# Weight tiles shared by two batches, low halves on VectorE, high halves of P on ScalarE, decoding moved behind attention

## The chip, the core and the metric

The kernel runs on one core of one Trainium2 chip. A time is the device time of one execution in microseconds (us). The profile adds one profiled execution: its span runs from the first to the last instruction, and its times are the ones that a sum can be made from. Engines are named as in the profile: PE (TensorE matmul), PEld (its weight loads), DVE (VectorE), ACT (ScalarE), POOL (GpSimd), SP (SyncE, which here issues every DMA).

## What is computed

Four batches of 448 positions go through three layers: causal attention with 12 heads of width 64; a low-rank mix over positions and a two-layer MLP of width 768 to 3072 to 768, with a residual; four small attention experts, of which each position uses two.

```python
scores = scale * q @ k.T; scores = where(causal mask, -1e9, scores)
x = softmax(scores) @ v                         # 4 batches, 12 heads, 448 x 64
u = x + (x.T @ U @ V).T                         # rank 32 over the 448 positions
x = u + relu(u @ w_ch1) @ w_ch2                 # 768 x 3072 and 3072 x 768
logits = x @ w_gate                             # 4 experts, 2 are kept for each position
out = sum over kept e of w[e] * (softmax(causal(x wq[e] (x wk[e]).T)) @ (x wv[e])) @ wo[e]
```

The inputs arrive as 64-bit floats.

## The kernel before, in words

**Numbers in two halves.** A value is kept as a high and a low fp16 half, and a product takes three matmuls (high·high, high·low, low·high; `PASS`). A unit of MLP work is one such product of 448 columns: 18 matmuls for one 128-row weight tile and one batch.

**Attention** (`attention(b)`) takes a batch in six pairs of heads. For a pair: scores on PE, a fused scale, mask and row maximum on DVE (the rows `CUSTOM_DVE_ANT_0` in the profile, `ISA` in the order), the exponential on ACT, the split of P into halves (`softmax`: the high half by a copy that `HIGH` gives to ACT or DVE for each of the four row blocks, the low half by a POOL subtraction), two DMA transposes, P·V on PE, another split and transpose, and the low-rank product (`lowrank`). That last one ends, for the pair, in a DVE instruction of 128x448 on a PSUM bank; the twelfth of these ends the attention of batches 0 and 1 and serves as a mark below.

**Weights.** The 48 MLP tiles (4 groups `g` of 6 first-layer and 6 second-layer tiles) come in as 64-bit floats, 768 KB each. `weight_tile(i, first)` with `first` decodes one: three DVE instructions of 128x768 on the integers (one TENSOR_SCALAR, two SCALAR_TENSOR_TENSOR), a square sum on ACT, a norm through a small matmul on PE, the high half on ACT, the scaled tile on ACT, the low half in two pieces of 384 columns on POOL, and a store of both halves to `W16` in device memory. Later uses load 384 KB from `W16`. Tiles live in a ring of `NW` slots; raw tiles in two buffers, decoded ones in three.

**The MLP** (`mlp(g, b)`) multiplies one group of tiles with one batch. The hidden values have one buffer, `HID`. Its PSUM banks are two ("f") until the experts' weights are made, three after.

**Order.** `ORDER` is the program order: `a` attention, `m` a batch and a group, `e` the experts of a batch. The instructions are only recorded. `Program.issue` then lists them, engine by engine, with a table of costs: of the instructions whose inputs are ready it takes the one with the smallest key. Attention and decoding have keys that grow with the pair (`HT` is half a pair; `first_key(i)` for tile `i`), MLP products have the large key `FILL`, so that they fill gaps, and evictions are `URGENT`. The result is a fixed order on each engine. Until `WARM_END` in its own reckoning it also places matmuls of zeros (line 953) where it sees PE idle. Every queue runs in order, SP's too, where loads, stores and transposes stand behind each other.

Of the kernel before, what the change touches and what calls it, by code (L numbers as in the profile page):

```python
# [30 lines left out]
HIGH = ("act", "act", "dve", "dve")  # L31
# [11 lines left out]
WARM_START, WARM_END, WARM_GAP = 3000.0, 130000.0, 100.0  # L43
NW = 19
# [3 lines left out]
ORDER = "a0 a1 m00 m01 m02 m03 e0 a2 m10 m11 m12 m13 e1 a3 m20 m21 m22 m23 e2 m30 m31 m32 m33 e3"  # L48
# [4 lines left out]
class Program:  # L53
# [7 lines left out]
    def __init__(self):  # L61
        self.ops = []
        self.key = 0.0
        self.group_op = None
        self.state = {}
        self.near = {}
        self.pitch = {}
        self.idle = None

# [54 lines left out]
    def cost(self, name, method, outs, ins, kw):  # L124
        o = outs[0]
        n = 1
        for c in o.shape[1:]:
            n *= c
        if name == "pe":
            f = 4.0 if ins[0].dtype == F32 else 1.0  # L130
            c = f * max(n / 2.4 + 2.5, 36.0)
            self.work = c * (ins[0].shape[0] / 128.0) * (o.shape[0] / 128.0)

            return c * (0.62 if HD in (o.shape[0], ins[0].shape[0]) and n >= C else 1.0)
        ptr = sum(x.free_size() == 1 and n > 1 for x in ins)
        psum = any(a.space == bass.MemoryType.PSUM for a in outs + ins)
        if name == "act" and method == "dma_start":
            return 300.0
        if name == "act":
            src = 51.0 if ins[0].space == bass.MemoryType.PSUM else 94.0  # L140
            return src + n / 1.2 + 93.0 * (ptr + len(outs) - 1)
        if name == "dve":
            m = 1
            for c in ins[0].shape[1:] if ins else o.shape[1:]:
                m *= c
            m = max(m, n)
            fast = not psum and method in ("tensor_scalar", "tensor_copy", "memset")
            two = not psum and n > 32 and (fast or sum(x.free_size() > 1 for x in ins) > 1)
            return ((64.0 + (m / 2 if fast else m)) / 0.96 + 64.0 * ptr) * (1.2 if two else 1.0)
        if name == "pool":  # L150
            if method == "partition_all_reduce":
                return 374.0
            return 148.0 + 1.89 * n if method == "tensor_tensor" else 260.0 + 2.5 * n
        return 350.0 + outs[0].nbytes() / 292.0 if method == "dma_start_transpose" else 650.0

    def add(self, name, method, fn, a, k):
# [4 lines left out]
        self.work = 0.0  # L161
        cost = self.cost(name, method, outs, ins, k)
        data = 0.0
        if method.startswith("dma"):
            nbytes = max(x.nbytes() for x in outs + ins)
            data = nbytes / (185.0 if method == "dma_start_transpose" else 360.0)
# [21 lines left out]
        if self.group_op:  # L188
            op = self.ops[-1]
            op["calls"].append((fn, a, k))  # L190
            op["cost"] += cost
            op["work"] += self.work
            op["deps"] |= deps
        else:
            op = dict(eng=name, cost=cost, data=data, deps=deps, calls=[(fn, a, k)], key=self.key,
                      work=self.work)
            self.ops.append(op)
            if self.group_op is False:
                self.group_op = True

    def issue(self):
# [9 lines left out]
        bus = 0.0  # L211
# [7 lines left out]
        while done < len(ops):  # L219
# [56 lines left out]
def kernel(  # L276
# [19 lines left out]
    for name, size in [  # L296
        ("uh", 2 * KD * S * 2), ("ul", 2 * KD * S * 2), ("x3", 2 * KD * S * 4),
        ("ring", NW * 3072), ("rd", RD), ("hid", GF * 2 * S * 2),
        ("stage", 2 * 3584), ("vs", NP * 2048), ("vh", 4096), ("p", 3 * PW * 4), ("phl", 2 * NBLK * 128 * 2 * 2),
        ("pt", 3 * 20 * C * 2), ("xhl", 2 * 2048), ("xtr", 2048),  # L300
        ("wv", 2 * 3120), ("tst", 256),
        ("idf", 512), ("one", 512), ("mask", S * 2), ("u3", 2 * NC * 2 * R * 2), ("vst", S * 2), ("id", 256),
        ("tie", 64), ("zero", 64), ("sm", SM * 4),
    ]:
        layout[name] = total
        total += size
# [14 lines left out]
    BANKS = {"s": (0, 1), "o": (2,), "l": (3, 4), "m": (5, 6, 7), "f": (5, 6), "r": (7,), "x": (5, 6), "y": (2, 7), "b": (3, 4)}  # L321
# [16 lines left out]
    HID = view("hid", 0, 128, F16, GF * 2 * S).rearrange("p (f l s) -> p f l s", f=GF, l=2)  # L338
# [10 lines left out]
    def hslot(r, o):  # L349
        return view(r, o, C, F16, 2 * NBLK * 128)  # L350

    SLOTS = [
        (P32[0:3] + [pslot("x3", 10752), pslot("x3", 10752 + 4480)], PHL[0:2] + [hslot("uh", 5376), hslot("ul", 5376)]),
        (P32[0:3], PHL[0:2]), (P32[0:3], PHL[0:2]), (P32[0:3], PHL[0:2]),
# [130 lines left out]
    def softmax(terms, nes, pts, last=False, kind="s", first=False):  # L485
# [4 lines left out]
        elif first:  # L490
            ps, hs = SLOTS[0]
# [28 lines left out]
        for j in range(2):  # L520
# [14 lines left out]
            sp.dma_start_transpose(out=PT[pts[j]], in_=h16[j])  # L535
# [26 lines left out]
    def weighted(vs, pts, y, dst, coef=None, kind="o"):  # L562
        shares(y, coef)
        t = psum(kind)
        with prog.group():
            for i, (lp, lv_) in enumerate(PASS):
                for j in range(NC):
                    for h, (va, pt) in enumerate(zip(vs, pts)):
# [4 lines left out]
                           PT[pt][0:C, k:k + kc * (NC - 1 - j) + 1:kc],  # L573
# [37 lines left out]
    def attention(b):  # L611
# [6 lines left out]
        for p in range(NP):  # L618
# [6 lines left out]
            if p == NP - 1 and b + 1 < B:  # L625
                v_scale(b + 1)
            i = n % 2
            prog.key = HT * 2 * n
            softmax([[(QK[i][64 * j:64 * j + 64, 1], QK[i][64 * j:64 * j + 64, 0])] for j in range(2)], -0.125,
                    [(2 * n + j) % 3 for j in range(2)], first=b == 0)  # L630
            prog.key = HT * (2 * n + 1)
            weighted([VH[:, 2 * i + j] for j in range(2)], [(2 * n + j) % 3 for j in range(2)], X3[b][:, p], XHL[i])
# [19 lines left out]
    kept = [False]  # L652

    def weight_tile(i, first):
# [76 lines left out]
    def mlp(g, b):  # L731
        if b == 0:
            factors(g)
        ut = (UH[b], UL[b])
        for f in range(GF):
            early = g + b + f == 0
            t = psum("m" if kept[0] else "f")
            wt = [a.rearrange("p (k m) -> p k m", k=KD) for a in tiles[2 * GF * g + f]]
            prog.key = FILL - early
            product(t[:, 0:S], [(wt[lw][:, k], ut[lx][:, k]) for k in range(KD) for lw, lx in PASS])  # L740
            prog.key = URGENT
            act.activation(t[:, 0:S], t[:, 0:S], AF.Relu, scale=(RF if b else RF0)[:, g * GF + f:g * GF + f + 1])
            act.activation(HID[:, f, 0], t[:, 0:S], AF.Copy)
            dve.tensor_tensor(out=HID[:, f, 1], in0=t[:, 0:S], in1=HID[:, f, 0], op=ALU.subtract)
        cf, ct = CF[g % 2], CTS[g % 2]
        dve.tensor_scalar(ct, PRS[:, g:g + 1], 2.0 ** 54 / HCAP, PU[:, b:b + 1], op0=ALU.mult, op1=ALU.mult)
        dve.tensor_scalar(cf, PW2[:, g * GF:g * GF + KD], 2.0 ** 83, ct, op0=ALU.mult, op1=ALU.mult)
        for d in range(KD):
            t = psum("m" if kept[0] else "f")
            wt = [a.rearrange("p (k m) -> p k m", k=GF) for a in tiles[2 * GF * g + GF + d]]  # L750
            prog.key = FILL
            product(t[:, 0:S], [(wt[lw][:, f], HID[:, f, lx]) for f in range(GF) for lw, lx in PASS])
            prog.key = URGENT
            dve.scalar_tensor_tensor(out=X3[b][:, d], in0=t[:, 0:S], scalar=cf[:, d:d + 1], in1=X3[b][:, d],
                                     op0=ALU.mult, op1=ALU.add)
            if g == NG - 1:
                absmax(AMX[:, b * KD + d:b * KD + d + 1], X3[b][:, d])

    def experts(b):
# [3 lines left out]
        free = 3072 * next(i for i in range(NW - 5) if not held & set(range(i, i + 6)))  # L763
        if last:
            qo, vo, yo, xo = ("hid", 0), ("ring", free), ("hid", 7168), ("ring", free + 4096)
# [6 lines left out]
        if last:  # L772
            OST = [view("ring", free + 6144 + i * 1792, 128, F32, S) for i in range(6)]
        else:
            OST = [view("rd", 14848 + i * 1792, 128, F32, S) for i in range(2)]
        pts = (0, 1, 2, 3) if last else (0, 1, 0, 1)
# [126 lines left out]
    zero_pads(SLOTS[0][1])  # L903
# [25 lines left out]
    def first_key(i):  # L929
        return HT * (1 + 0.9 * i if i < 2 * GF else 12 + (i - 2 * GF) / 3)  # L930

    def group(b, g):
        for i in range(2 * GF * g, 2 * GF * (g + 1)):
            prog.key = URGENT if b else first_key(i)
            weight_tile(i, not b)
        mlp(g, b)
# [13 lines left out]
    for step in ORDER.split():  # L950
        kind, b = step[0], [int(c) for c in step[1:]]
        {"a": attention, "m": group, "e": moe}[kind](*b)
# [47 lines left out]
```

## Time and profile before

| | |
|---|---|
| median of 3 runs | 1176.02 us (1173.72 to 1176.1) |
| the profiled execution's own time | 1177.93 us |
| its span | 1176.2 us, so 1.7 us lie around it |
| busy in the span: PE, DVE, ACT, POOL | 1088.9, 678.1, 546.7, 371.3 us |
| mean granted TensorE clock | 0.967 of full speed |
| DMA | 192.57 MB, 164 GB/s on average |

A row by groups reads: line, engine, operation, output<-input, shapes, count | busy us, mean ns of one | idle us of the engine just before them. A row by stretches gives busy us of each engine with its count of instructions, the granted clock and the mean busy share of the 16 DMA engines. Nearly every instruction has line 250, because the recorder issues it there; so rows are told apart by engine, operation and shape.

### The profile page before, as it was taken

How to read it: one execution, taken by the hardware profiler on the slowest of the kernel's cores; microseconds unless marked ns; L12 is line 12 of the kernel's file. 1: busy time of each engine (PE TensorE's matmuls, PEld its weight loads, DVE VectorE, ACT ScalarE, POOL GpSimd, SP SyncE). 2: the span in 40 equal slices, each digit the busy share in tenths (PEclk: the TensorE clock that was granted, in tenths of full speed). 3: DMA queues.
4: the chain of work that ended last, by engine and by line, in shares of the span. 5: the costliest groups of instructions: out<-in, count | busy, mean ns of one | idle time of the engine just before them, and what ended most of it. 6: DMA issues, size and time to landing. Idle time of an engine off the chain costs nothing.

```text
span 1176.2 us, 18782 instructions
## 1 busy us (share of the span) xinstructions
PE 1088.9 (93%) x6888; PEld 571.7 (49%) x6888; DVE 678.1 (58%) x1831; ACT 546.7 (46%) x1317; POOL 371.3 (32%) x419
## 2 busy tenths in 40 slices
PE   7899969979988999999999999999999997899895
PEld 3454434434444455445555554455555544355452
DVE  8869888998889765665432555654224333111453
ACT  4755767676577544575412456652122323121142
POOL 3755755766453102454200034540000012000012
PEclk9999978998999999999999999999999998999998
DMA  7887888897786754998734349984443255331023
GB/s 195 208 195 245 211 199 242 260 229 206 230 265 222 239 189 112 213 231 200 175 108 120 96 107 216 234 180 118 122 121 108 82 131 112 125 121 54 1 40 87
DMA packets 220141, 192.57 MB, mean 164 GB/s; under 512 B 176304, under 2 KB 179504, under 8 KB 220048
## 3 DMA queue, kind: packets, MB, share of 16 engines
q1 hardware_dynamic: 220048, 191.36, 61.0%
q8 instruction: 54, 0.88, 0.3%
q14 instruction: 39, 0.32, 0.1%
HBM read 121.60 MB, written 26.74 MB: 126 GB/s over the span
## 4 chain that ended last, share of the span: by engine, by line
PE 65%; DVE 9%; issue 3%; ACT 3%; DMA 2%; POOL 2%; POOLq 0%; SPq 0%; DVEq 0%; ACTq 0%
PE bank L250 65%; DVE arena L250 9%; ACT arena L250 2%; POOL arena L250 2%; DMA arena<-in_v_dram 1%; DMA arena<-in_w_dram 0%; DMA arena<-in_we_dram 0%; DMA arena<-w 0%; ACT bank L250 0%; POOLq L995 0%; SPq L250 0%; DVEq L250 0%; ACTq L250 0%; POOLq L250 0%
## 5 line engine op out<-in xcount | busy, mean ns | idle before, releaser
L250 PE MATMUL bank<-arena 128*128 128x448 f16 (+12 forms) x6496 | 1006.5, 332 | 70.0 <-DVE arena L250 40.8
L250 PEld LDWEIGHTS <-arena 128*128 128x128 f16 (+4 forms) x5960 | 489.2, 106 | 489.8 <-issue 124.9
L250 POOL TENSOR_TENSOR arena<-arena 112x336 f16<-112x336 f32 (+6 forms) x408 | 369.1, 924 | 796.2 <-ACT arena L250 719.6
L250 ACT ACTIVATE arena<-arena 128x768 f16<-128x768 f32 (+10 forms) x671 | 376.6, 591 | 282.8 <-DVE arena L250 267.6
L250 DVE TENSOR_TENSOR arena<-bank,arena 128x448 f16<-128x448 f32 (+2 forms) x160 | 95.4, 600 | 215.2 <-ACT arena L250 183.4
L250 DVE CUSTOM_DVE_ANT_0 arena<-bank,arena 112x112 f32<-112x112 f32 (+4 forms) x280 | 125.7, 475 | 62.6 <-PE bank L250 55.1
L250 ACT ACTIVATE bank<-bank,arena 128x448 f32<-128x448 f32 x96 | 57.8, 603 | 222.8 <-PE bank L250 221.8
L250 DVE SCALAR_TENSOR_TENSOR arena<-bank,arena 128x448 f32<-128x448 f32 (+1 forms) x120 | 73.4, 614 | 148.0 <-PE bank L250 125.0
L250 DVE SCALAR_TENSOR_TENSOR arena<-arena 128x768 int32<-128x768 int32 (+5 forms) x159 | 154.9, 993 | 5.3 <-ACT arena L250 4.2
L250 ACT ACTIVATE arena<-bank 128x448 f16<-128x448 f32 (+2 forms) x160 | 82.6, 523 | 74.7 <-PE bank L250 72.8
L250 DVE TENSOR_SCALAR arena<-arena 128x1 f32<-128x1 f32 (+9 forms) x367 | 90.7, 267 | 20.1 <-ACT arena L250 9.7
L953 PE MATMUL bank<-arena 128*128 128x448 f16 x392 | 89.8, 376 | 13.4 <-DVE arena L250 12.4
L250 DVE CAST arena<-arena 112x336 f16<-112x336 f32 (+2 forms) x160 | 85.4, 547 | 2.1 <-PE bank L250 1.0
L250 PEld LDWEIGHTS bank<-arena 64*112 64x112 f32 (+5 forms) x536 | 49.4, 176 | 55.9 <-issue 18.9
L953 PEld LDWEIGHTS <-arena 128*128 128x128 f16 x392 | 39.1, 105 | 54.3 <-issue 25.9
L250 DVE TENSOR_REDUCE arena<-arena 128x1 f32<-128x448 f32 (+7 forms) x107 | 58.2, 546 | 9.5 <-DMA arena<-in_v_dram 5.2
L250 ACT ACTIVATION_READ_ACCUMULATOR arena<-arena 112x1 f32 (+1 forms) x304 | 57.0, 188 | 0.0
L250 ACT ACTIVATE arena<-bank,arena 64x128 f16<-64x128 f32 (+3 forms) x85 | 34.2, 405 | 44.6 <-PE bank L250 38.7
L250 DVE TENSOR_TENSOR arena<-arena 112x8 f16<-112x8 f32 (+4 forms) x69 | 24.6, 368 | 1.4
L250 DVE DVE_READ_ACCUMULATOR2_ANT arena<- 112x1 f32 (+1 forms) x280 | 22.7, 81 | 0.0
L250 DVE TENSOR_SCALAR arena<-bank 128x1 f32<-128x1 f32 x48 | 7.2, 149 | 12.8 <-PE bank L250 12.7
L250 DVE RECIPROCAL arena<-arena 112x8 f32<-112x8 f32 (+1 forms) x36 | 7.0, 195 | 0.7
(12 smaller groups left out, 13.6 us busy)
## 6 DMA issues: line engine op xcount, KB each, us to landing
arena<-w SPq DMA_DIRECT2D x162, 384.0 KB, 3.3
arena<-in_w_dram SPq DMA_DIRECT2D x48, 768.0 KB, 5.6
w<-arena SPq DMA_DIRECT2D x54, 384.0 KB, 3.1
arena<-in_qk_dram SPq DMA_DIRECT2D x24, 448.0 KB, 5.6
arena<-in_v_dram SPq DMA_DIRECT2D x24, 224.0 KB, 5.0
out_dram<-arena SPq DMA_DIRECT2D x24, 224.0 KB, 2.6
arena<-in_we_dram SPq DMA_DIRECT2D x6, 384.0 KB, 4.6
arena<-arena SPq DMA_TRANSPOSE x88, 4.6
```

What stands on the lines that cost most here:

```text
L250: fn(*a, **k)
L953: prog.idle = lambda: nc.tensor.matmul(bank[:, 7, 64:512], ZERO.to_broadcast([128, 128]), ZERO.to_broadcast([128, S]), start=True, stop=True)
```

## The change

Four things are changed together, and some sizes with them.

- **Two batches on one group of tiles.** `mlp(g, bs)` takes a list of batches, and a group is loaded or decoded once for steps that follow each other. In `ORDER` a step now reads group, then batches: `m00 m01` is group 0 for batch 0 and then batch 1, `m101` group 1 for both. `HID` gets a second buffer; to pay for it the ring shrinks from 19 to 15 slots.
- **Decoding behind attention.** `first_key` spreads the first 12 tiles over all twelve pairs and puts the other 36 after the last pair. Both attentions of batches 0 and 1 use the spare buffers for P. Matmuls of zeros may be placed until 210 in place of 130 (us, in the planner's reckoning). MLP steps recorded between attention 1 and expert step 0 use four PSUM banks, two of them shared with the scores.
- **The low half of a decoded tile** is formed on DVE by one SCALAR_TENSOR_TENSOR from the decoded tile (`split`, which was there already); the ACT pass that scaled the tile and the two POOL pieces go.
- **The high halves of P** are all copied on ACT.
- The planner's table of costs now keeps DVE instructions that read two operands from SBUF, or run at their fast rate, apart from POOL instructions.

```diff
-HIGH = ("act", "act", "dve", "dve")
+HIGH = ("act", "act", "act", "act")
-WARM_START, WARM_END, WARM_GAP = 3000.0, 130000.0, 100.0
-NW = 19
+WARM_START, WARM_END, WARM_GAP = 3000.0, 210000.0, 100.0
+NW = 15
-ORDER = "a0 a1 m00 m01 m02 m03 e0 a2 m10 m11 m12 m13 e1 a3 m20 m21 m22 m23 e2 m30 m31 m32 m33 e3"
+ORDER = "a0 a1 m00 m01 m101 m20 m30 e0 a2 m21 m31 e1 a3 m02 m12 m22 m32 e2 m03 m13 m23 m33 e3"
...
+            if o["port"]:
+                t = max(t, port)
+                port = t + cost
...
-        (P32[0:3], PHL[0:2]), (P32[0:3], PHL[0:2]), (P32[0:3], PHL[0:2]),
+        (P32[0:3] + [pslot("hid", 10752), pslot("hid", 10752 + 4480)], PHL[0:2] + SPARE, PT[0:3]),
+        (P32[0:3], PHL[0:2], PT[0:3]), (P32[0:3], PHL[0:2], PT[0:3]),
...
-        act.activation(hi, t, AF.Copy, scale=s)
-        act.activation(t, t, AF.Copy, scale=s)
-        for j in range(2):
-            cols = slice(384 * j, 384 * j + 384)
-            pool.tensor_tensor(out=lo[:, cols], in0=t[:, cols], in1=hi[:, cols], op=ALU.subtract)
+        split(hi, lo, t, s)
         sp.dma_start(out=W16[i], in_=both)
...
-    def mlp(g, b):
-        if b == 0:
+    def mlp(g, bs):
+
+        if 0 in bs:
             factors(g)
...
+        bank = "m" if kept[0] else "g" if started[0] else "f"
         for f in range(GF):
+            for b in bs:
...
     def first_key(i):
-        return HT * (1 + 0.9 * i if i < 2 * GF else 12 + (i - 2 * GF) / 3)
+        return HT * (1 + 2.0 * i if i < 2 * GF else 25 + (i - 2 * GF) / 3)
...
+    def group(g, bs):
+        if last_group[0] != g:
+            for i in range(2 * GF * g, 2 * GF * (g + 1)):
+                prog.key = URGENT if g in made else first_key(i)
+                weight_tile(i, g not in made)
...
+        mlp(g, bs)
```

SP's queue in the second half of attention 1 (batch 1), before. `in_w_dram` is a raw tile's load, `w<-arena` the store of a decoded one, the 128x20x112 transposes belong to P and the 128x8x128 ones to the low-rank step:

```order
L250 DMA arena<-in_v_dram 112x512
L250 DMA_TRANSPOSE arena<-arena 128x8x128
L250 DMA w<-arena 128x1536
L250 DMA arena<-in_w_dram 128x768
L250 DMA_TRANSPOSE arena<-arena 128x20x112
L250 DMA w<-arena 128x1536
L250 DMA arena<-in_w_dram 128x768
L250 DMA_TRANSPOSE arena<-arena 128x20x112
L250 DMA w<-arena 128x1536 x2
L250 DMA arena<-in_w_dram 128x768
L250 DMA arena<-in_qk_dram 128x896
```

And in the change, the last pairs of attention 1 and what follows them:

```order
L252 DMA_TRANSPOSE arena<-arena 128x20x112 x2
L252 DMA_TRANSPOSE arena<-arena 128x8x128
L252 DMA arena<-in_w_dram 128x768 x2
L252 DMA w<-arena 128x1536 x2
L252 DMA_TRANSPOSE arena<-arena 128x8x128
L252 DMA arena<-in_v_dram 112x512
L252 DMA arena<-in_w_dram 128x768
L252 DMA arena<-in_v_dram 112x512
L252 DMA w<-arena 128x1536
L252 DMA arena<-in_w_dram 128x768
L252 DMA w<-arena 128x1536
L252 DMA arena<-in_w_dram 128x768 x2
```

Most loads and stores of tiles moved from between the transposes to behind the last of them.

DVE in a pair of attention 1, before: an eviction of a hidden tile (TENSOR_TENSOR on a bank), two copies of P's high half (CAST with four dimensions), the small steps of a tile's norm (128x1) and of the row sums (112x8):

```order
L250 TENSOR_TENSOR arena<-bank,arena 128x448
L250 TENSOR_SCALAR arena<-arena 128x1
L250 CAST arena<-arena 112x2x3x56
L250 TENSOR_TENSOR arena<-bank,arena 128x448
L250 TENSOR_SCALAR arena<-bank 128x1
L250 TENSOR_SCALAR arena<-arena 112x8
L250 TENSOR_SCALAR arena<-arena 128x1
L250 RECIPROCAL arena<-arena 112x8
L250 CAST arena<-arena 112x2x4x56
```

In the change, in the last pair of attention 1 (ISA on a bank is the fused mask and maximum):

```order
L252 ISA arena<-bank,arena 112x448
L252 ISA arena 112x1
L252 SCALAR_TENSOR_TENSOR arena<-arena 128x768
L252 TENSOR_SCALAR arena<-arena 128x768
L252 TENSOR_SCALAR arena<-arena 112x8
L252 SCALAR_TENSOR_TENSOR arena<-arena 128x768
L252 SCALAR_TENSOR_TENSOR arena<-bank,arena 32x128
L252 TENSOR_TENSOR arena<-bank,arena 128x448
L252 RECIPROCAL arena<-arena 112x8
```

No copy of P stands on DVE any more, and a tile has three SCALAR_TENSOR_TENSOR of 128x768 where it had two.

ACT in a late pair of attention 1, in the change (112x2x3x56 and 112x2x4x56 are the high halves that DVE had; before, ACT had 128x768 passes of tiles and evictions of hidden tiles at this place):

```order
L252 ACTIVATE arena<-arena 112x2x2x56
L252 ACTIVATE arena<-arena 112x2x3x56
L252 ACTIVATE arena<-arena 112x448
L252 ACTIVATE arena<-bank,arena 64x128
L252 ACTIVATE arena<-bank,arena 32x128
L252 ACTIVATE arena<-arena 112x448
L252 ACTIVATE arena<-arena 112x2x3x56
L252 ACTIVATE arena<-arena 112x112
L252 ACTIVATE arena<-arena 112x2x4x56
L252 ACTIVATE arena<-arena 112x336
```

All four copies of P's high half now queue between the exponentials.

## Rows read from the trace of the kernel before

**Rows 1.** Page, busy time by engine, and DVE in 40 slices.
```profile
PE 1088.9 (93%) x6888; PEld 571.7 (49%) x6888; DVE 678.1 (58%) x1831; ACT 546.7 (46%) x1317; POOL 371.3 (32%) x419
DVE  8869888998889765665432555654224333111453
```

**Rows 2.** Stretches, before 345, to 432, to the end.
```profile
0.00:345.00 345.00, 294.97 (x1886) 151.28 (x1887) 294.81 (x776) 227.62 (x523) 204.95 (x209) 0.93 0.82 221
345.00:432.00 87.00, 79.85 (x426) 41.05 (x425) 67.35 (x147) 46.71 (x75) 20.66 (x20) 1.00 0.70 239
432.00:1177.00 745.00, 714.06 (x4580) 379.39 (x4577) 315.94 (x910) 272.36 (x722) 145.65 (x190) 0.98 0.51 128
```

**Rows 3.** Stretches of 25 us: one with MLP products alone.
```profile
1025.00:1050.00 25.00, 25.00 (x134) 12.92 (x132) 3.91 (x7) 5.44 (x10) 0.00 (x0) 1.00 0.40 124
```

**Rows 4.** The chain that ended last: start us, us, what.
```profile
391.40 159.20 PE bank L250 x1096
...
983.64 10.51 issue
...
1003.09 4.17 DMA arena<-w
```

**Rows 5.** PE groups by shape, 0 to 432.
```profile
L250 PE MATMUL bank<-arena 128*128 128x448 f16 x962 | 201.7, 361 | 20.1 <-DVE arena L250 18.3 <-ACT arena L250 1.6
L953 PE MATMUL bank<-arena 128*128 128x448 f16 x392 | 89.8, 376 | 13.4 <-DVE arena L250 12.4 <-DVE arena L897 1.0
...
L250 PE MATMUL bank<-arena 128*128 128x1 f32 x96 | 16.3, 239 | 5.3 <-ACT arena L250 4.8 <-DVE arena L250 0.2
```

**Rows 6.** DVE timeline: the mark, the twelfth low-rank instruction.
```profile
345.42 0.68 DVE L250 CUSTOM_DVE_ANT_0 arena<-bank,arena 128x448 f32<-128x448 f32 x1
```

**Rows 7.** DVE groups by shape, 0 to 345.
```profile
L250 DVE SCALAR_TENSOR_TENSOR arena<-arena 128x768 int32<-128x768 int32 x82 | 93.9, 1146 | 0.6
L250 DVE TENSOR_SCALAR arena<-arena 128x768 int32<-128x768 int32 x41 | 31.2, 760 | 7.0 <-DMA arena<-in_w_dram 3.7 <-POOL arena L250 2.8 <-issue 0.2
L250 DVE CAST arena<-arena 112x448 f16<-112x448 f32 x24 | 18.1, 758 | 0.0
...
L250 DVE CAST arena<-arena 112x336 f16<-112x336 f32 x24 | 14.1, 591 | 0.0
...
L250 DVE TENSOR_SCALAR arena<-arena 128x1 int32<-128x1 int32 x88 | 12.5, 144 | 0.4
...
L250 DVE TENSOR_TENSOR arena<-bank,arena 128x448 f16<-128x448 f32 x18 | 11.0, 616 | 3.1 <-ACT arena L250 3.0
```

**Rows 8.** DVE groups by shape, 398 to 426.
```profile
L250 DVE SCALAR_TENSOR_TENSOR arena<-arena 128x768 f16<-128x768 f32 x6 | 5.9, 1011 | 1.0 <-ACT arena L250 1.0
```

**Rows 9.** ACT groups by shape, 0 to 345.
```profile
L250 ACT ACTIVATE arena<-arena 128x768 f16<-128x768 f32 x79 | 69.5, 883 | 46.7 <-DVE arena L250 46.6
...
L250 ACT ACTIVATE arena<-arena 112x448 f32<-112x448 f32 x24 | 15.8, 660 | 4.0 <-DVE arena L250 4.0
L250 ACT ACTIVATE arena<-arena 112x336 f32<-112x336 f32 x24 | 13.6, 565 | 8.1 <-DVE arena L250 8.1
```

**Rows 10.** ACT groups by shape, 0 to 391: a high half of two blocks.
```profile
L250 ACT ACTIVATE arena<-arena 112x224 f16<-112x224 f32 x24 | 9.0, 375 | 0.0
```

**Rows 11.** POOL groups by shape, 0 to 345.
```profile
L250 POOL TENSOR_TENSOR arena<-arena 128x384 f16<-128x384 f32 x76 | 85.7, 1149 | 68.2 <-ACT arena L250 68.2
```

**Rows 12.** DMA, 0 to 345: queue, packets, MB, share of 16 engines; issues.
```profile
q1 hardware_dynamic: 83320, 75.73, 82.1%
...
arena<-in_w_dram SPq DMA_DIRECT2D x42, 768.0 KB, 5.7
...
arena<-arena SPq DMA_TRANSPOSE x36, 4.9
```

**Rows 13.** DMA, 600 to 660, where tiles alone are loaded.
```profile
q1 hardware_dynamic: 2435, 6.65, 37.3%
...
arena<-w SPq DMA_DIRECT2D x17, 384.0 KB, 3.1
```

**Rows 14.** DVE timeline: first instruction of a tile's decoding, first and last of seven.
```profile
325.45 0.56 DVE L250 TENSOR_SCALAR arena<-arena 128x768 int32<-128x768 int32 x1 [0.82 <-DMA arena<-in_w_dram]
...
375.66 0.54 DVE L250 TENSOR_SCALAR arena<-arena 128x768 int32<-128x768 int32 x1
```

More of the change, by code (lines that the diff above doesn't have):

```diff
@@ L68, in __init__ @@
         self.idle = None
+        self.port = False
     def engine(self, name, eng):
@@ L147, in cost @@
             fast = not psum and method in ("tensor_scalar", "tensor_copy", "memset")
-            two = not psum and n > 32 and (fast or sum(x.free_size() > 1 for x in ins) > 1)
-            return ((64.0 + (m / 2 if fast else m)) / 0.96 + 64.0 * ptr) * (1.2 if two else 1.0)
+            self.port = not psum and n > 1 and (fast or sum(x.free_size() > 1 for x in ins) > 1)
+            return (64.0 + (m / 2 if fast else m)) / 0.96 + 64.0 * ptr + 80.0 * (self.port and n > 32)
         if name == "pool":
@@ L337 @@
     DEC = [view("rd", 12288 + i * 3072, 128, F32, 768) for i in range(3)]
-    HID = view("hid", 0, 128, F16, GF * 2 * S).rearrange("p (f l s) -> p f l s", f=GF, l=2)
+    HID = [view("hid", i * 10752, 128, F16, GF * 2 * S).rearrange("p (f l s) -> p f l s", f=GF, l=2) for i in range(2)]
     QK = [view("stage", i * 3584, 128, F32, 2 * S).rearrange("p (t s) -> p t s", t=2) for i in range(2)]
@@ L483, in scaled_copy, with softmax @@
             dve.tensor_scalar(o, a, scale, None, op0=ALU.mult)
-    def softmax(terms, nes, pts, last=False, kind="s", first=False):
+    def softmax(terms, nes, pts, last=False, kind="s", slots=None):
         ps, hs = P32[0:3], PHL[0:2]
@@ new lines, in mlp @@
+            for b in bs:
+                early = g + b + f == 0
+                t = psum(bank)
+                wt = [a.rearrange("p (k m) -> p k m", k=KD) for a in tiles[2 * GF * g + f]]
+                prog.key = FILL - early
+                ut = (UH[b], UL[b])
+                product(t[:, 0:S], [(wt[lw][:, k], ut[lx][:, k]) for k in range(KD) for lw, lx in PASS])
+                hid = HID[b % 2]
+                prog.key = URGENT
+                act.activation(t[:, 0:S], t[:, 0:S], AF.Relu, scale=(RF if b else RF0)[:, g * GF + f:g * GF + f + 1])
+                act.activation(hid[:, f, 0], t[:, 0:S], AF.Copy)
+                dve.tensor_tensor(out=hid[:, f, 1], in0=t[:, 0:S], in1=hid[:, f, 0], op=ALU.subtract)
@@ new lines, in mlp @@
+        cf, ct = [[a[b % 2] for b in bs] for a in (CF, CTS)]
+        for i, b in enumerate(bs):
+            dve.tensor_scalar(ct[i], PRS[:, g:g + 1], 2.0 ** 54 / HCAP, PU[:, b:b + 1], op0=ALU.mult, op1=ALU.mult)
+            dve.tensor_scalar(cf[i], PW2[:, g * GF:g * GF + KD], 2.0 ** 83, ct[i], op0=ALU.mult, op1=ALU.mult)
+        for d in range(KD):
+            for i, b in enumerate(bs):
+                t = psum(bank)
+                wt = [a.rearrange("p (k m) -> p k m", k=GF) for a in tiles[2 * GF * g + GF + d]]
+                hid = HID[b % 2]
+                prog.key = FILL
+                product(t[:, 0:S], [(wt[lw][:, f], hid[:, f, lx]) for f in range(GF) for lw, lx in PASS])
+                prog.key = URGENT
+                dve.scalar_tensor_tensor(out=X3[b][:, d], in0=t[:, 0:S], scalar=cf[i][:, d:d + 1], in1=X3[b][:, d],
+                                         op0=ALU.mult, op1=ALU.add)
+                if g == NG - 1:
+                    absmax(AMX[:, b * KD + d:b * KD + d + 1], X3[b][:, d])
@@ L762, in experts @@
         held = {(ring_n[0] - 1 - i) % NW for i in range(NE)}
-        free = 3072 * next(i for i in range(NW - 5) if not held & set(range(i, i + 6)))
+        two = 3072 * next(i for i in range(NW - 1) if not held & {i, i + 1})
         if last:
-            qo, vo, yo, xo = ("hid", 0), ("ring", free), ("hid", 7168), ("ring", free + 4096)
+            qo, vo, yo, xo = ("hid", 0), ("ring", two), ("hid", 7168), ("ring", two + 4096)
         else:
@@ L772, in experts @@
         if last:
-            OST = [view("ring", free + 6144 + i * 1792, 128, F32, S) for i in range(6)]
+            OST = [view("hid", 10752 + i * 1792, 128, F32, S) for i in range(6)]
         else:
             OST = [view("rd", 14848 + i * 1792, 128, F32, S) for i in range(2)]
-        pts = (0, 1, 2, 3) if last else (0, 1, 0, 1)
+        pts = PT if last else PT[0:2] * 2
         ks, ko, kl = "xyy" if last else "sll" if b == B - 2 else "sol"
```

79 lines of the change are left out of this document (34 added, 45 removed).

## The prediction

> **What bounds the kernel now.** I read the page first, and in it the engines' shares beside DVE's 40 slices [rows 1]: PE is busy for 93% of the span, yet DVE, 58% on the whole, stands at eighths in the first third and at two to six tenths later. The kernel has regimes, and the mean tells of none. So the next view was the table by stretches [rows 2], cut at the mark: the twelfth low-rank instruction on DVE, at 345.4 [rows 6], which ends the attention of batches 0 and 1. Up to there DVE works 294.8 of 345 us, 85%, and the DMA engines 82%. PE's 295 us are padding in part: 392 products of zeros, 89.8 us [rows 5], and what PE waits for in these groups is mostly DVE. From 432 on, where the first value product of the experts stands, PE works 714 of 745 us and DVE 316.
>
> Is PE really full there? A stretch with nothing but MLP work has 134 products in 25.00 us [rows 3], 186.6 ns for 448 columns, at granted clock 1.00, the 2.4 GHz level. The chain [rows 4] says the same: from 391.4 it lies on PE for 159 us in one piece, and it leaves PE later for small pieces, such as 10.5 us of issue at 983.6 and 4.2 us of a weight load at 1003. The kernel is thus a first stage of 391 us bound by DVE and DMA, and then PE's own sum. Time is to be won only by ending the first stage earlier with no more left to PE.
>
> **The first stage, up to the mark.** I counted in the order of each program what stands ahead of the twelfth low-rank step. On DVE: 128x768 SCALAR_TENSOR_TENSOR 82 before and 44 now (30 of decoding, 14 new low halves), TENSOR_SCALAR 41 and 16, copies of P 48 and none, 128x1 steps 191 and 83, hidden and bank evictions down by 23. At the means of [rows 7]: 52 x 1.146 + 25 x 0.760 + 24 x (0.758 + 0.591) + 108 x 0.144 + 23 x 0.616 = 141 us go. The new low half has the price of the same operation from f32 to f16 halves, 1.011 [rows 8]: 14 us come. Net 127; since DVE's means overlap (count times mean over all its groups is 340 for 295 busy), 110 to 127 of busy time, and DVE falls from 295 to 168 to 185.
>
> ACT loses 86 of its 128x768 passes at 0.883 [rows 9], and gains the 48 copies of P's high half. Half-width copies cost 0.375 there [rows 10]; the full exponential of the same shape costs 0.565 to 0.660 [rows 9]; I take 0.565 of these ends as the mean of the two widths, 27 us. With its evictions gone too, ACT falls from 228 to about 170. POOL loses the 76 pieces of 128x384, 86 of its 205 us [rows 11]; nobody waits for that unless ACT and DVE are idle, so I cost it at nothing, hidden behind both.
>
> DMA: 82.1% of 345 is 283 us of all 16 engines [rows 12]. In the stretch where tiles alone are loaded, 17 loads of 384 KB take 37.3% of 60 us [rows 13], 1.32 us each, so 2.63 for a raw tile of 768 KB. In SP's queue 25 raw loads and 24 stores move from ahead of the last low-rank transpose to behind it (the 42 raw loads of [rows 12] become 16 or 17): 25 x 2.63 + 24 x 1.32 = 97 us, and DMA falls to 186. These transfers stood between the transposes of P in the same queue, which are 36 of 4.9 us [rows 12] and do not change in number.
>
> PE: MLP-shaped products ahead of the mark fall from 552 to 156, but zeros ahead of it grow from 392 to some 465. At 0.210 and 0.229 us each (201.7 / 962 and 89.8 / 392 [rows 5]) the rest of PE's 295 was 295 - 116 - 90 - 7 (44 norms of 0.17 that move) = 82. Now: 82 + 33 + 106 = 221, or, with both at 0.187 [rows 3], 198. The zeros were meant for gaps, but they stand in order, and now they are half of what PE does there.
>
> So DMA asks 186, DVE up to 185, PE 198 to 221. At the pace of before, where the busiest reached 0.855 of the stage, 186 gives 217 and 198 gives 232. The floor is 198, without any wait. At 0.774, DVE's share between 345 and 432 [rows 2], DMA's 186 would give 240. I take **225** for the mark, in place of 345, with 198 and 240 as its ends: 19 us for each of the twelve pairs of heads, where it was 29.
>
> **From the mark to the first value product.** The price of that gain stands here: 36 tiles are decoded behind attention, where only a few were. Up to that value product the order has 966 MLP-shaped products before (962 in the trace, [rows 5]) and 1383 now; after the mark that leaves 1383 - 156 = 1227, x 0.1866 = 229, and with 36 norms at 0.17 [rows 5], 235. PE was busy 79.85 of 87 us between 345 and 432, and 0.958 from 432 on [rows 2]. I take 0.95, as products for two batches on one tile give PE twice the work for each decoded tile: **247**, with ends 235 and 256. DVE's load here is 32 tiles of about 4.5 us (0.760 + 2 x 1.146 + 1.011 and small steps), 144, and some evictions, under 190 of 247.
>
> **From the value product to the end.** Now 744 us (1176.2 - 432). The products brought forward, 1383 - 966 = 417, are gone from here: 417 x 0.1866 = 78, which leaves **666**. Loads of decoded tiles fall from 162 to 138 by sharing; at a mean DMA share of 0.51 [rows 2] they were hidden, so this is nothing. The smaller ring (15 for 19) makes loads wait longer for a slot; its cover is that PE now uses each tile for 36 products, 6.7 us, against a transfer of 3.1 [rows 13]. The high halves on ACT lie open only in the softmax of the last experts, where DVE had been idle: from 0, where ACT waits for DVE anyway, to 4.4; I take 2. The second buffer for `HID` is a gain of at most the few us that PE waits for ACT [rows 5]; nothing.
>
> A rule speaks against the term of 78. The Trainium skill, Perfetto Trace Analysis, section Identifying the Most-Contended Engine, says that a busy matmul row is no measure of how near TensorE is to its limit, and that the busy share of the weight loads is one. By it PEld's 12.92 of 25 us [rows 3] means an engine half used, the 417 products would be worth perhaps 39, and the sum would be 39 more. The row holds against it: clock 1.00 and one column for each 2.4 GHz cycle, so the term stands at 78.
>
> **Sum.** 225 + 247 + 666 + 2 = 1140 of span, against 1176.2. The profiled execution took 1177.93, 1.7 beyond its span and 1.9 over the median of 1176.02: the two cancel within 0.2, so **1140 us** as a median, 36 less.
>
> **The rivals.**
> *Decoding paces the second stage.* The seven tiles that begin between 325.45 and 375.66 [rows 14] do so 8.4 us apart, though attention no longer loads DVE much after 345. Kept up for the 32 tiles left, that is 268, and 14 for the last tile's products: 282 for 247, 1175. For it: two raw buffers and three decoded ones are unchanged, and ACT waits 46.6 us for DVE before its tile passes [rows 9]. Against: POOL's two pieces (2.3 us a tile) and one ACT pass leave the chain of a tile, and DMA asks 2.63 + 1.32 = 4 a tile. Half of that delay gives 1157. Chance 0.16.
> *What is brought forward is not given back.* With 417 products fewer as filling, the holes of the last part (10.5 of issue, 4.2 of loading [rows 4]) grow, at each of the four expert steps, by up to 10 us: half of 78, 1140 + 39 = 1179 at worst and 1160 in the middle. Against: 714 of 745 leaves only 31 us idle with the filling there [rows 2]. Chance 0.13. The rule of the Trainium skill cited above (Perfetto Trace Analysis, Identifying the Most-Contended Engine) would end at the same 1179 by another way.
> *Slower: the chain of a pair sets the pace.* Exponential, all four high halves and evictions queue on ACT, then POOL's low halves, transposes, P·V. If a pair takes 22 us in place of 19, the mark is at 261 and everything is lost (225 + 36). At 24 it is at 288: 1203. For it: ACT waits before its exponentials for DVE [rows 9], so latency counts there already, and 106 us of zeros can stand ahead of late work. Against: a pair's 29 us now holds 25 of DVE work, and 10 of them go. Chance 0.11.
> *The attention stage runs without waits.* Mark at 198, 1113. Chance 0.07.
>
> **How the numbers follow.** My forecast has 0.53, with 1118 to 1160 as its own range (198 to 240 at the mark, 235 to 256 behind it, not all at one end). The range 1105 to 1176 adds the fast case, most of the first two rivals, and leaves out the slower one and edges, under 2 in 10. A change of less than 0.2%, 2.4 us, can hardly be told from none here. Slower takes the third rival and the worst end of the second, 0.13; same 0.04 from the ends of the first two; faster the rest, 0.83.
>
> **What would show it.** In the trace after: the twelfth low-rank instruction at 225 (198 to 240); up to there DVE about 175 busy, ACT 170, DMA 186, POOL without 128x384. The first value product near 472, with PE full before it at clock 1.00 and raw tiles less than 7 us apart: 8 says the first rival. From there to the end 666; more says the second. I am wrong if the mark comes after 255, or if PE shows gaps behind it that begin at a tile.

## The result and the profile after

The change takes 1136.62 us (median of 4 runs, 1135.03 to 1138.64) against 1176.06 for the kernel before (4 runs); the ratio is 0.9668, interval 0.9648 to 0.9689. The forecast was 1140. The profiled execution took 1136.78, with a span of 1135.1.

The table by stretches of the kernel after, cut at the same two events as [rows 2] (the twelfth low-rank instruction on DVE, the first value product on PE):

```profile
0.00:214.50 214.50, 203.06 (x1502) 106.34 (x1503) 173.60 (x527) 159.39 (x434) 113.01 (x133) 0.99 0.89 220
214.50:456.10 241.60, 240.93 (x1314) 128.31 (x1313) 194.36 (x422) 107.89 (x186) 0.00 (x0) 1.00 0.58 200
456.10:1135.10 679.00, 637.13 (x4158) 339.85 (x4156) 265.01 (x804) 289.12 (x777) 143.70 (x190) 0.97 0.52 129
```

The three stages last 214.5, 241.6 and 679.0 us, where 225, 247 and 666 were forecast; before, they took 345, 87 and 744. The page's slices show the same: DVE's eighths, which filled the first third in [rows 1], have spread thinner over the first two stages, and PE is at nine tenths or more in nearly every slice from the second on:

```profile
PE   8999999999999999999899999999999987999895
DVE  6798788978888884454546454642124340211443
```

PE's slices before, where the first third holds sixes to nines:

```profile
PE   7899969979988999999999999999999997899895
```

What the first stage holds now, by groups of DVE and PE, up to about the mark:

```profile
L252 DVE SCALAR_TENSOR_TENSOR arena<-arena 128x768 int32<-128x768 int32 x30 | 33.0, 1106 | 0.0
L252 DVE SCALAR_TENSOR_TENSOR arena<-arena 128x768 f16<-128x768 f32 x14 | 15.2, 1084 | 0.5 <-ACT arena L252 0.4
L252 DVE TENSOR_SCALAR arena<-arena 128x768 int32<-128x768 int32 x16 | 10.9, 685 | 0.0
...
L983 PE MATMUL bank<-arena 128*128 128x448 f16 x462 | 101.7, 362 | 1.3 <-DVE arena L914 1.0 <-DVE arena L252 0.2
L252 PE MATMUL bank<-arena 128*128 128x448 f16 x162 | 34.2, 352 | 1.4 <-DVE arena L252 1.2
```

And the issues of DMA there (count, KB, us to landing), with the queue's share:

```profile
q1 hardware_dynamic: 76348, 46.83, 88.6%
...
arena<-in_w_dram SPq DMA_DIRECT2D x17, 768.0 KB, 6.1
...
arena<-arena SPq DMA_TRANSPOSE x36, 4.5
```

The 82 decoding steps of [rows 7] are 30, the 42 raw loads of [rows 12] 17, no copy of P is on DVE, and zeros take 101.7 us of PE.

Where the last stage waits, from the chain of the kernel after, 496 to 606 (experts of batch 0 and attention of batch 2):

```profile
498.06 6.37 DMA arena<-arena
...
526.90 6.52 DMA arena<-arena
...
537.80 4.68 DMA arena<-arena
...
554.75 7.10 DMA arena<-arena
```

DMA into and out of the same tile store is a transpose, of P or of the low-rank step. PE's waits for 496 to 606, and then for 665 to 744 (attention of batch 3), by what ended them (us in total, times, longest):

```profile
PE bank L252 <- DMA arena<-arena: 5.8, 3, 2.5
...
PE bank L252 <- DMA arena<-arena: 4.5, 5, 2.0
```

The shape of the waiting matmul tells which transpose it is: 128x128 products (128\*64) are the low-rank step's, 112x448 ones (112\*64) are P·V. The first line is from 496 to 606, the other two from 665 to 744:

```profile
L252 PE MATMUL bank<-arena 128*64 128x128 f16 x72 | 5.1, 220 | 5.8 <-DMA arena<-arena 5.8
...
L252 PE MATMUL bank<-arena 112*64 112x448 f16 x36 | 7.9, 365 | 2.4 <-DMA arena<-arena 2.4
...
L252 PE MATMUL bank<-arena 128*64 128x128 f16 x52 | 3.8, 220 | 2.2 <-DMA arena<-arena 2.2
```

So 8.0 of the 10.3 us are waits for the low-rank step's transposes. Before, PE had no wait for a transpose between 432 and 968, where the attention of batches 2 and 3 lies.

### The profile page after: what moved, and what is told of

It reads as the page before. It is cut to its first block, busy times and chain, and to the rows that moved or that the text cites. A ratio compares the mean times of both kernels' runs of the same rounds, so it can differ in the third digit from the quotient of the medians.

```text
span 1135.1 us, 18755 instructions
## 1 busy us (share of the span) xinstructions
PE 1081.1 (95%) x6970; PEld 574.5 (51%) x6970; DVE 633.0 (56%) x1751; ACT 556.4 (49%) x1397; POOL 256.7 (23%) x323
## 4 chain that ended last, share of the span: by engine, by line
PE 67%; DMA 9%; ACT 4%; POOL 2%; issue 2%; DVE 1%; SPq 0%; POOLq 0%; ACTq 0%; DVEq 0%
PE bank L252 66%; DMA arena<-arena 6%; ACT arena L252 4%; POOL arena L252 2%; DVE arena L252 1%; DMA arena<-w 1%; DMA out_dram<-arena 1%; DMA arena<-in_wv_dram 1%; DMA arena<-in_we_dram 0%; SPq L252 0%; PE bank L983 0%; POOLq L1025 0%; ACT bank L252 0%; POOLq L252 0%; ACTq L252 0%
## 5 line engine op out<-in xcount | busy, mean ns | idle before, releaser
L252 PE MATMUL bank<-arena 128*128 128x448 f16 (+10 forms) x6496 | 989.0, 328 | 48.7 <-DMA arena<-arena 24.1
L252 ACT ACTIVATE arena<-arena 128x768 f16<-128x768 f32 (+11 forms) x751 | 390.0, 556 | 255.8 <-DVE arena L252 230.1
L252 POOL TENSOR_TENSOR arena<-arena 112x112 f16<-112x112 f32 (+5 forms) x312 | 254.5, 835 | 869.3 <-ACT arena L252 862.7
L252 DVE SCALAR_TENSOR_TENSOR arena<-arena 128x768 int32<-128x768 int32 (+5 forms) x207 | 189.5, 935 | 8.1 <-ACT arena L252 7.0
L252 DVE CUSTOM_DVE_ANT_0 arena<-bank,arena 112x448 f32<-112x448 f32 (+4 forms) x280 | 125.0, 476 | 73.6 <-PE bank L252 60.9
L983 PE MATMUL bank<-arena 128*128 128x448 f16 x474 | 104.2, 361 | 1.3 <-DVE arena L914 1.0
L252 DVE TENSOR_SCALAR arena<-arena 128x1 int32<-128x1 int32 (+9 forms) x367 | 79.6, 242 | 27.6 <-ACT arena L252 16.3
L252 DVE TENSOR_REDUCE arena<-arena 128x1 f32<-128x448 f32 (+6 forms) x107 | 57.5, 546 | 6.4 <-DMA arena<-in_v_dram 3.5
L252 ACT ACTIVATE arena<-bank,arena 64x128 f16<-64x128 f32 (+2 forms) x85 | 34.4, 406 | 49.8 <-PE bank L252 43.2
L252 DVE TENSOR_SCALAR arena<-bank 128x1 f32<-128x1 f32 x48 | 7.3, 153 | 17.1 <-PE bank L252 11.6
L252 DVE CAST arena<-arena 112x8 f16<-112x8 f32 x32 | 14.9, 465 | 0.7 <-PE bank L252 0.5
```

Of the source, the lines that this page charges most:

```text
L252: fn(*a, **k)
L983: prog.idle = lambda: nc.tensor.matmul(bank[:, 7, 64:512], ZERO.to_broadcast([128, 128]), ZERO.to_broadcast([128, S]), start=True, stop=True)
```

## The experiments

The theory was the prediction's own: each stage ends with its fullest engine, sharing hides decoding behind attention. Its rivals were that single parts make the gain in another way: the order, the pair's chain on ACT, the matmuls of zeros. Marks and first value products below are the same two events as above. Each run is compared with the kernel before on the same chip; the ratios can be set beside the change's 0.9668. The last three columns are of one profiled execution each: those of x_high (1178.56 us) and x_share (1174.27) are among the longest of ten, that of x_gap600 (1129.19) is the shortest of five. Every edit also changes the fixed order that the planner lists, so a difference between two runs holds this too.

| kernel | ratio (interval) | median, us | mark | first value product | end of span |
|---|---|---|---|---|---|
| the change | 0.9668 (0.9648 to 0.9689) | 1136.62 | 214.5 | 456.1 | 1135.1 |
| x_high | 1.0017 (0.9992 to 1.0042) | 1173.38 | 254.0 | 496.6 | 1176.7 |
| x_pool | 0.9630 (0.9593 to 0.9667) | 1131.62 | 224.8 | 457.8 | 1129.5 |
| x_key | 0.9885 (0.9843 to 0.9927) | 1158.77 | 242.8 | 483.1 | 1155.4 |
| x_share | 0.9979 (0.9957 to 1.0000) | 1168.64 | 216.7 | 427.3 | 1172.5 |
| x_zero0 | 0.9736 (0.9702 to 0.9770) | 1141.84 | 223.5 | 466.2 | 1139.6 |
| x_high_zero0 | 0.9825 (0.9786 to 0.9863) | 1154.82 | 229.0 | 473.0 | 1152.7 |
| x_slots | 0.9686 (0.9651 to 0.9722) | 1135.75 | 227.2 | 463.6 | 1131.8 |
| x_cost | 0.9739 (0.9710 to 0.9768) | 1143.34 | 221.3 | 460.5 | 1141.9 |
| x_gap600 | 0.9672 (0.9648 to 0.9696) | 1133.84 | 209.6 | 448.9 | 1127.5 |
| x_pool_gap600 | 0.9578 (0.9554 to 0.9602) | 1122.36 | 216.0 | 448.6 | 1123.1 |
| x_key_zero0 | 0.9886 (0.9862 to 0.9910) | 1158.60 | 234.0 | 480.3 | 1156.0 |
| x_nw13 | 0.9634 (0.9607 to 0.9660) | 1129.23 | 214.7 | 453.3 | 1128.8 |

**Sharing undone (x_share).**

```diff
-ORDER = "a0 a1 m00 m01 m101 m20 m30 e0 a2 m21 m31 e1 a3 m02 m12 m22 m32 e2 m03 m13 m23 m33 e3"
+ORDER = "a0 a1 m00 m10 m20 m30 e0 a2 m01 m11 m21 m31 e1 a3 m02 m12 m22 m32 e2 m03 m13 m23 m33 e3"
```

> The change with each group of tiles used by one batch at a time (groups 0 to 3 for batch 0, then its experts, attention of batch 2, groups for batch 1, and so on), so tiles decoded behind attention serve 18 products each before they leave. Theory (sharing is what hides decoding): behind the mark 32 tiles at 5.5 to 6 us pace PE, which has only about 810 x 0.187 = 151 us of products for them; first value product at 390 to 405 with PE gaps of 25 to 35 us, time 1155 to 1175. Rival (decoding is quicker than PE even for one batch): first value product at 370 to 380 and PE full, time 1132 to 1145.

The time came out as the theory has it, 1168.64. The first value product came at 427, later than 390 to 405. The stretch behind the mark, and PE's waits in it:

```profile
216.70:427.30 210.60, 177.51 (x915) 90.45 (x913) 178.32 (x396) 96.96 (x166) 0.00 (x0) 0.95 0.69 233
...
PE bank L252 <- DVE arena L252: 24.2, 14, 6.4
PE bank L252 <- ACT arena L252: 8.6, 8, 3.1
```

PE is idle for 33.1 of 210.6 us and waits for DVE and ACT, for decoding or for evictions that stand behind it, where the change idles 0.7 of 241.6. The longest wait, 6.43 us, is of the second kind, and the decoding itself had waited for a raw tile (two rows of DVE, one of PE):

```profile
300.29 0.70 DVE L252 TENSOR_SCALAR arena<-arena 128x768 int32<-128x768 int32 x2 [3.18 <-DMA arena<-in_w_dram]
...
303.88 1.15 DVE L252 TENSOR_TENSOR arena<-bank,arena 128x448 f16<-128x448 f32 x2
...
304.55 0.91 PE L252 MATMUL bank<-arena 128*128 128x448 f16 x2 [6.43 <-DVE arena L252]
```

The idle time is most of the loss against the change: the two profiled spans are 37.4 us apart, the two medians 32. The rest is PE's own work, 8.7 us longer in all (granted clock 0.95 in this stretch, for 1.00), less 4.9 us of idle time that the last part saves. With sharing undone, the change, its decoding still behind attention, gains next to nothing (0.9979). What sharing gives is work for PE beside the decoding: 1223 MLP-shaped products for 31 raw tiles in the change, 836 for the same 31 here. Not every tile has two users, though. By `ORDER`, only groups 0 and 1 serve both batches before the first value product (36 products for a tile); the 24 tiles of groups 2 and 3 are decoded there for batch 0 alone (18), and batch 1 loads them again.

**Copies of P back on DVE (x_high).**

```diff
-HIGH = ("act", "act", "act", "act")
+HIGH = ("act", "act", "dve", "dve")
```

> The change with two of the four high halves of P back on DVE. Theory (each stage ends with its fullest engine): up to the mark DVE gains 24 x (0.758 + 0.591) = 32 us on its 174, 206 for a stage of 215, so it becomes one of the fullest; the mark comes at 220 to 235, and the time is 1140 to 1155. Rival (the chain of a pair, in which ACT does exponentials and all copies, sets the pace): ACT loses 27 us, the mark comes before 215 and the time is 1120 to 1135.

Both sides missed: the mark came at 254, and the whole gain was gone. Up to the mark, by stretch and by groups:

```profile
0.00:254.00 254.00, 234.39 (x1636) 119.80 (x1637) 190.44 (x567) 141.89 (x383) 109.20 (x133) 0.97 0.72 180
...
L252 DVE CAST arena<-arena 112x448 f16<-112x448 f32 x24 | 18.8, 817 | 0.0
L252 DVE CAST arena<-arena 112x336 f16<-112x336 f32 x24 | 12.5, 557 | 0.0
L983 PE MATMUL bank<-arena 128*128 128x448 f16 x599 | 135.2, 373 | 15.8 <-DVE arena L252 14.8 <-DVE arena L914 1.0
```

DVE, at 190 of 254, is no fuller than in the change (174 of 214.5). What has grown is PE, 234, with 599 zeros, 33 us more of them: the planner places them where it sees PE idle. So zeros became a suspect.

The last line holds more than busy time: PE was idle for 15.8 us in front of zeros, 14.8 of them waiting for DVE, where the change has 0.2. In the kernel the zeros write the PSUM bank into which the norm of a decoded tile goes. Seven waits make up the 14.8 us, and each ends within 0.1 us of the end of a DVE instruction that reads a norm out of its bank. The longest, DVE and then PE:

```profile
211.75 0.14 DVE L252 TENSOR_SCALAR arena<-bank 128x1 f32<-128x1 f32 x1
...
211.94 0.54 PE L983 MATMUL bank<-arena 128*128 128x448 f16 x2 [3.65 <-DVE arena L252]
```

So a zero can stand in PE's order and wait for decoding, with attention's own matmuls behind it.

**Zeros taken away, with copies on ACT and on DVE (x_zero0, x_high_zero0).** Both have the edit below; the second also has that of x_high.

```diff
-WARM_START, WARM_END, WARM_GAP = 3000.0, 210000.0, 100.0
+WARM_START, WARM_END, WARM_GAP = 3000.0, 0.0, 100.0
```

> The change without any matmul of zeros. Theory Z (the 462 zeros ahead of the mark, 102 us of PE, stand in order ahead of attention's own matmuls and hold it up): the mark comes earlier, at 190 to 208, time 1115 to 1130. Theory C (the chain of a pair over DVE, ACT, POOL and the transposes sets the pace, zeros fall into its gaps and keep the granted clock up): mark at 215 to 235 with a clock under 0.9 there, time 1136 to 1155.

> Two of four high halves of P on DVE, and no zeros. In the run with them on DVE the mark came 39 us later than in the change, with 137 more zeros ahead of it (33 us) and 31 us of copies more on DVE. Theory Z (the zeros, set by the planner's own reckoning, made those 39 us): mark at 205 to 225, within 10 us of the same kernel without zeros and with all copies on ACT. Theory C (the copies stand in the pair's chain): mark 30 to 45 later than that kernel's, time 25 to 45 more than its.

```profile
0.00:223.50 223.50, 149.13 (x1021) 82.66 (x1022) 176.48 (x540) 160.33 (x435) 119.52 (x133) 0.82 0.89 225
```

```profile
0.00:229.00 229.00, 155.15 (x1006) 85.75 (x1007) 188.77 (x573) 141.01 (x385) 116.54 (x133) 0.81 0.81 207
```

These two rows are the first stretch of x_zero0 and of x_high_zero0. With copies on ACT, zeros gain 9 us at the mark (223.5 to 214.5), with a clock of 0.99 against 0.82: the numbers of theory C. With copies on DVE the zeros cost 25 (229.0 to 254.0): theory Z, with a mark 4 us beyond its bound. So of the 39.5 us between x_high and the change at the mark, 5.5 remain without zeros (229.0 - 223.5), and of the whole 37 us 13 remain. In x_high the waits of DVE and ACT for PE were 27.2 and 34.9 us up to the mark, against 11.8 and 18.8 in the change and 11.6 and 20.8 in x_high_zero0: PE, behind its zeros, came late. How much of the 25 us is the zeros' own time and how much their waits for DVE, no run separates; zeros in a bank of their own would.

**The old keys (x_key, x_key_zero0).** The second has no zeros either.

```diff
-        return HT * (1 + 2.0 * i if i < 2 * GF else 25 + (i - 2 * GF) / 3)
+        return HT * (1 + 0.9 * i if i < 2 * GF else 12 + (i - 2 * GF) / 3)
```

> The change with the old keys of decoding, so that all 48 tiles are decoded among the attention of batches 0 and 1. Theory: some 25 tiles go back ahead of the mark, 97 us of DMA on 192 and about 110 of DVE on 174; mark at 300 to 325, with about 400 more products ahead of it (75 us that are missing later): time 1155 to 1175. Rival (the gain came from the lighter work of DVE and from sharing, not from the place of decoding): the mark stays under 260, time 1130 to 1145.

> The old keys of decoding, without zeros. With the 612 zeros (131 us) that the planner puts in with these keys the mark came at 242.8, 28 later than in the change. Theory Z (the zeros made those 28): mark at 222 to 232, within 8 of the change without zeros (223.5), time 1140 to 1150. Rival (early tiles themselves hold the attention up): mark at 240 to 255, time 1155 to 1172.

The time of x_key, 1158.77, was in the theory's range, but not for its reason: the mark came at 242.8, not 300 to 325, and only 20 raw tiles were loaded ahead of it, not some 40. That the ring of 15 slots holds decoding back there, because a shared tile stays until both batches have used it, fits this and was not tested alone. Its 612 zeros (131.2 us) are part of the later mark: without them it is 234.0, still 10.5 behind x_zero0, above the 232 of theory Z. The time did not move at all (0.9886); the clock fell to 0.79. So the place of decoding is worth 1.5% without zeros (0.9886 to 0.9736) and 2.2% with them.

**The low half back on POOL (x_pool).**

```diff
-        split(hi, lo, t, s)
+        act.activation(hi, t, AF.Copy, scale=s)
+        act.activation(t, t, AF.Copy, scale=s)
+        for j in range(2):
+            cols = slice(384 * j, 384 * j + 384)
+            pool.tensor_tensor(out=lo[:, cols], in0=t[:, cols], in1=hi[:, cols], op=ALU.subtract)
```

> The change with the low half of a decoded tile formed as before (an ACT pass that scales, two POOL pieces). Theory: up to the mark only 14 tiles are concerned, and behind it PE is full at 99.7% with DVE at 194 of 242, so little moves: mark 212 to 220, first value product 455 to 465, time 1132 to 1143. Rival (the longer chain of a tile, 2 x 1.15 on POOL and 0.88 on ACT, starves PE behind attention): gaps on PE between 215 and 457, time 1148 to 1165.

The rival fell: behind the mark PE is busy 232.74 of 233.0 us. The mark came later than expected, 224.8, but with 216 MLP products ahead of it in place of 162, and the first value product came where it was. The time, 1131.62, is just under the expected range. This part of the change gained nothing; undone, the kernel is at 0.963, its interval overlapping the change's a little.

**Buffers, ring and costs (x_slots, x_nw13, x_cost).** The third puts back the old table of costs, with its dearer transposes, and takes out the shared `port`; its edit is not shown.

```diff
-        (P32[0:3] + [pslot("hid", 10752), pslot("hid", 10752 + 4480)], PHL[0:2] + SPARE, PT[0:3]),
+        (P32[0:3], PHL[0:2], PT[0:3]),
```

```diff
-NW = 15
+NW = 13
```

> The change with before's buffers for attention of batch 1: three P and two pairs of halves, no spare ones. Theory C (latency of a pair's chain counts, so pairs must overlap): the six pairs of batch 1 take 2 to 4 us more each, mark at 225 to 240, time 1145 to 1162. Rival (buffers are not waited for, the engines' loads set the pace): mark 212 to 220, time 1133 to 1141.

> The change with a ring of 13 slots. Theory (slots are not what the end waits for: the 12 us of idle PE that the last part has more stand in the attention of batches 2 and 3): last part within 4 us of 679, time 1133 to 1142. Rival (loads wait for slots): 1148 to 1165, with PE waiting for loads of tiles after the first value product.

> The change with the planner's old table of costs. The computation is the same, only the order of instructions differs. Theory C (work taken out of the chain and out of SP's queue made the gain): 1133 to 1146. Rival (the planner's new costs, which keep DVE and POOL apart and price transposes lower, made much of it): 1150 to 1175.

Without the spare buffers the mark comes at 227.2, as the theory says, and the time does not change, as the rival says: 206 MLP products stand ahead of that mark, and the last part is 668.2. Two slots fewer cost nothing; 1129.23 is even below the expected range, its last part 675.5 long. The ring is not what the last part waits for. The old costs are 0.7% slower (0.9739 against 0.9668), by the order that they give.

**Fewer zeros (x_gap600, x_pool_gap600).** The second also has the edit of x_pool.

```diff
-WARM_START, WARM_END, WARM_GAP = 3000.0, 210000.0, 100.0
+WARM_START, WARM_END, WARM_GAP = 3000.0, 210000.0, 600.0
```

> The change with zeros only in gaps that the planner sees as longer than 0.6 us: 328 in place of 474. With all copies on ACT, no zeros at all cost 9 us at the mark (clock 0.82), and with half of them on DVE the 599 zeros cost 25. Theory (zeros keep the clock up, but past a number they hold attention up): mark at 203 to 212, clock over 0.93, time 1124 to 1134. Rival (the zeros fall into gaps, and DMA at 0.89 sets the pace): mark 213 to 220, time 1135 to 1143.

> The low half of a decoded tile on POOL again, and zeros only in gaps over 0.6 us (293). It is the candidate for the fastest. Theory: the mark comes 3 to 10 earlier than the 224.8 of the same kernel with all zeros, time 1120 to 1129. Rival (DMA at 0.93 sets the pace there): mark 222 to 228, time 1130 to 1137.

First stretches, x_gap600 and then x_pool_gap600:

```profile
0.00:209.60 209.60, 184.16 (x1365) 96.52 (x1366) 173.28 (x528) 159.28 (x434) 113.29 (x133) 0.98 0.91 225
```

```profile
0.00:216.00 216.00, 190.25 (x1367) 99.86 (x1368) 165.47 (x530) 170.77 (x450) 142.50 (x163) 0.95 0.94 230
```

With 328 zeros in place of 462 ahead of the mark, PE falls from 203 to 184 us, the clock stays at 0.98, and the mark comes 4.9 us earlier, in one execution each; the time's interval does not tell it from the change. Together with the low half on POOL it does: 0.9578, and 1122.36 us is the fastest kernel here, with an interval clear of the change's. Both marks are as the theories said. DMA is then at 0.94 of the first stage, the fullest of all engines there; whether it sets the pace that is left, no run tests.

## Why the prediction was right, by its steps

**The first stage.** The loads came as counted: DVE 173.6 (168 to 185), ACT 159 (about 170), DMA 0.89 x 214.5 = 191 (186), POOL 113, PE 203 (198 to 221). Only the pace was better than taken: DMA reached 0.89 and PE 0.95 of the stage, where the 0.855 of before had been taken, so 214.5 for 225. PE's share is padding by half, as the count of zeros had it, and x_high shows what the step left out: how many zeros there are hangs on the planner's reckoning, and they can cost what they were to win, by their time and by their waits for DVE. The copies of P had no price of their own in the sum beyond the loads of DVE and ACT. They carry 13 us without zeros and 37 with the planner's: without this edit the change would not have been faster.

**Behind the mark.** 1223 products were there, 1227 were counted. PE was busy 240.9 of 241.6 us, 0.997 where 0.95 was taken, but its work was 240.9 and not 235: the first error is 12 us and the second 6 the other way, so 241.6 for 247. The reason given, products for two batches on one tile, holds for the tiles of groups 0 and 1 only; the 24 of groups 2 and 3 had one batch there. It was enough: x_share, with one batch on all, leaves PE standing for 33 us.

**The last stage.** The work went as forecast: PE's busy time fell from 714.06 [rows 2] to 637.13, 76.9 us for 78. The rule cited from the Trainium skill (Perfetto Trace Analysis, Identifying the Most-Contended Engine), priced as the prediction did by the weight loads alone, though the page sets the matmuls' FLOPs against the peak beside them, would have put this term at half; here the row held.

What was too low is idle time: 679.0 - 637.1 = 41.9 us now against 30 before. Of these 12, 10.3 (5.8 + 4.5) are PE waiting for transposes in the attention of batches 2 and 3, most of them the low-rank step's. That has the form of the second rival, at 12 us for its 39, but at other places: the holes grew in the attention beside and behind the first two expert steps, and not at the last two, where PE idles 11.3 and 18.1 us (906 to 963, 1071.5 to the end) after 11.7 and 18.1 before (968 to 1016, 1112 to the end). That filling is missing fits two rows: before, DMA was as full in places (0.89 from 500 to 560, 1.02 from 720 to 760) and PE waited for no transpose there; and x_share, which keeps 2893 of these products for the last stage where the change has 2506, waits 1.5 us for the low-rank transposes where the change waits 8.0. But x_share idles 37.0 us there in all, and no run changes the filling alone, so the cause is not shown. It is not the ring (x_nw13), nor the copies: the last stage of x_high idles 43.6. The ring's cover, as the prediction gave it, was wrong even so: in this stage every step serves one batch, so a tile has 18 products and not 36. The smaller ring cost nothing that x_nw13 shows.

**The sum.** 10.5 and 5.4 too high, 13 too low, and 2 for late copies that no run shows: these nearly cancel, so by luck the total is better than its terms. The first rival did not happen, and would have, in part, without sharing. The slower rival's price was about right: it set the loss of everything at a mark of 261, and x_high, at 254, is even with the kernel before; but zeros and copies on DVE did it there, not ACT's chain.

**Left open.** Why x_nw13 is no slower but seems faster; how much of x_key is the ring's doing; what made the transposes of the last stage late; and what sets the pace of the first stage when the zeros are few.

## What to carry to other kernels

Cut the span at events, not at times, sum each engine in each stage, and say what the next stage pays for what the first gives up: here decoding moved behind attention left PE idle for only 0.7 us, because sharing half of the tiles gave PE enough to do there. Padding that a planner places by its own reckoning is work in order like any other; when another edit lengthens its gaps it can eat the gain, so test edits with and without it, and look at what the padding itself waits for. Undo parts one at a time even when the whole is as forecast: one part was worth nothing, and the fastest kernel here is the change without it and with fewer zeros.

## What the runs showed of the hardware

The granted clock without zeros was 0.82 over the first stage, a mean of stretches at 2.4 and at 1.2 GHz (1.00 from 184 to 186, 0.50 from 188 to 190); with 328 zeros it was 0.98 and with 462 it was 0.99. Yet with that clock the mark came only 9 to 14 us earlier: without zeros PE is busy for 149 of 223.5 us there and waits for others in the rest.

DVE's decoding steps are quicker where POOL is silent. Behind the mark, the change (POOL 0 us) and then x_pool (POOL 73 of 233 us):

```profile
L252 DVE SCALAR_TENSOR_TENSOR arena<-arena 128x768 int32<-128x768 int32 x66 | 62.4, 951 | 0.1
L252 DVE TENSOR_TENSOR arena<-bank,arena 128x448 f16<-128x448 f32 x34 | 21.0, 619 | 5.6 <-ACT arena L252 5.4
```

```profile
L252 DVE SCALAR_TENSOR_TENSOR arena<-arena 128x768 int32<-128x768 int32 x60 | 63.2, 1054 | 0.3
...
L252 DVE TENSOR_TENSOR arena<-bank,arena 128x448 f16<-128x448 f32 x33 | 20.1, 619 | 11.0 <-ACT arena L252 10.8
```

With two operands in SBUF the step takes 951 and 1054 ns, and 1146 in [rows 7]; the eviction with one operand in PSUM takes 619 in both. The Trainium skill, SBUF — State Buffer, section Who interferes with whom, says that a DVE instruction with two SBUF inputs contends with a GpSimd instruction that reads SBUF, and that one with at most one SBUF input does not, outside the two-port modes; these rows agree.
